# Gated attention and low-rank mixer on one core: batch 0 turns other score blocks by DMA, and the loads of the weights and of batch 1 are placed anew

## The chip, the core and the metric

The kernel runs on one core of one Trainium2 chip. The metric is the device time of one execution in microseconds (us). The engines are TensorE (PE; its weight loads are listed as PEld), VectorE (DVE), ScalarE (ACT), GpSimd (POOL) and SyncE (SP). SP, ACT and POOL also issue DMAs, each in the order of its own queue.

## The reference

Eight batches of 3136 rows. The first stage is attention without a softmax: scores of z with itself, rectified and squared, times v, gated by u. The second is a mixer: a low-rank product along the sequence, then a two-layer network along the channels, each added back.

```python
scores = (1.0 / S) * np.matmul(z, z.transpose(0, 2, 1))   # z: (8, 3136, 64)
attn = np.maximum(scores, 0.0) ** 2                       # symmetric
x = u * np.matmul(attn, v)                                # u, v: (8, 3136, 256)
xt = x.transpose(0, 2, 1)
h = xt @ U @ V                                            # U: (3136, 32), V: (32, 3136)
u2 = x + h.transpose(0, 2, 1)
out = u2 + np.maximum(u2 @ w_ch1, 0.0) @ w_ch2            # 256 -> 1024 -> 256
```

## The kernel before

**Tiles and blocks.** The 3136 rows are 24 tiles of 128 rows and a tail of 64, called tile 24. A score *block* is 128 rows by 128 columns in bf16 (32 KB); `q` holds 296 of them (`NBLK`). For output tile c the kernel needs the blocks (j, c) of all j: 24 matmuls of 128x256 (L1053, `av`) into one PSUM bank, `acc`. The tail's output is 50 smaller matmuls (L1068), turned into shape by one more (L1078). VectorE then gates the result with u into `xc` (L1086, `gate`): this is the *output* of the tile. The outputs of a batch have positions 0 to 24; the tail's stands at position `AT24`.

**How a block is made.** `score` (L1025) multiplies pieces of zT (z transposed, kept twice over the partitions) into a PSUM `pair` of 1024 columns; ACT (L1040) or DVE (L1042) rectifies it into `q`; DVE squares it (L1046). One such piece is a *unit*. Since the scores are symmetric, (c, j) can also be had by turning (j, c): SP issues a DMA transpose (L1049, `q<-q`; `q<-TJ` for the tail). There are three pairs and two accumulators.

**Batch 0** starts cold, and works in groups of four tiles; `DIRECT` gives the limit of each group. A tile c makes its row up to the limit, in pieces of at most 8 blocks, and turns these blocks; the blocks with a tile at or beyond the limit are made twice, once for each side. Groups that `DIRECT` does not name have the limit 24: everything is turned. For the first group the limit is 0: each pair of rows j is made for its four columns at once, the rows from 4 up to `FLIP` are also turned (*flips*), and the blocks beyond `FLIP` are made when that tile comes. Later batches turn everything.

**Mixer.** Each batch's mixer runs beside the next batch's attention: `t1` (L1095, with U), `t1s` (L1112), `h` (L1133, with V), the sum u (L1144), its cast to `ubf` and a DMA transpose to `uT` (L1161), `w1` (L1171), its rectification (L1182, L1184), `w2` (L1197, L1190), the output sum (L1209) and the store (L1214, POOL).

**Loads.** For batch 0, SP and ACT load z (L898, tail L902) and SP most of v (L940); half of v comes by POOL as bf16 (L947), after a one-element copy (L953) that waits for the cast of v that `GATE_V` names. From batch 1 on, all loads are issued by ACT: z in four pieces (cast at L912 and L914 into two buffers `zbf`, the tail in `zbt`, then DMA transposes at L923 into `zT`), v in 13, u in 13 (L967, tail L970). The weights are loaded once by ACT: U at L984 and L988, V at L993, w1 at L978, w2 at L981. Each load has a *gate*, an output of the batch before (of batch 0, for the weights) after which it may go; the numbers are positions. `WAT` gives those of the weights, `Z_AT` the first of z; v starts at position 9. A load from batch 1 on, or of a weight, also takes one of four tokens (`tok`) for as long as the planner thinks it in flight.

**The order** of the whole program is written before it runs, by a planner in Python (`make_plan`, `Plan.run`). It plays a list schedule with costs for each task and emits each engine's instructions in the order so found. `T_BLK` and `T_ROW` are its prices of a transposed block and of a loaded row tile. On PE, `select` takes units of up to `LOOK` positions ahead of the output that is being made, first `av` tasks in their order, and mixer tasks whenever these have fallen behind by `HOLD` (in the last batch `HOLD_LAST`) of a batch. On the chip the engines keep this order and wait for what they need; a wrong price in the planner becomes a wait.

Of the kernel before, what the change touches and what calls it, by code (L numbers as in the profile page):

```python
# [17 lines left out]
NT = 24  # L18
# [4 lines left out]
NBLK = 296  # L23
NXC = 7
NPAIR, NACC = 3, 2
LOOK = 8


DIRECT = (0, 16, 20)

WAT = [(n, 3 + k // 3) for k, n in enumerate((8, 9, 10, 11, 0, 1, 2, 3, 4, 5, 6, 7))]
Z_AT = 5
GATE_V = 1

FLIP = 12
SOFT = 5
NEAR = 2
ACCS = 3
AT24 = 4
HOLD = 0.03  # L40
HOLD_LAST = 0.16

# [52 lines left out]


L_PE, L_EW, L_TR, L_DMA = 0.36, 0.08, 1.3, 2.2  # L100
T_BLK, T_ROW = 0.2, 0.37


class Plan:
# [203 lines left out]
def make_plan():  # L308
    pl = Plan()
    for name, n in (  # L310
        ("xc", NXC), ("pair", NPAIR), ("acc", NACC), ("stg", 6), ("us", 3),
        ("zbf", 2), ("zT", 2), ("v", 2), ("TJ", 1), ("o24", 1), ("u24", 1), ("x24", 2), ("u32", 3), ("ubf", 1), ("uT", 2),
        ("r1", 7), ("r24", 1), ("ob", 2), ("t1", 2), ("t1f", 1), ("tok", 4),
    ):
        pl.pool(name, n)
    pl.free_at["DVE"] = 1.5
# [3 lines left out]
    after = lambda b, pos: out_done.get((b, pos))  # L320
    wts = [[] for _ in range(12)]
    tok = lambda on: [Ref("tok")] if on else []
# [5 lines left out]
    for b in range(NB):  # L328
# [4 lines left out]
        for p, (z0, nb) in enumerate(pieces):  # L333
            st, zbf = Ref("stg"), Ref("zbf")
            ld = add(
                f"zld{b}.{p}", {"ACT": 0.5} if b else {("SP", "ACT")[p % 2]: 0.45},
                lambda K, t, b=b, z0=z0, nb=nb, st=st: K.load_z(t, b, z0, nb, st),
                deps=[after(b - 1, Z_AT + p)] if b else [], prio=0.45 if b else 0.1 * p, pipe=0.1 * nb,
                alloc=[st] + tok(b), behind=zl[-1:],
            )  # L340
            zl.append(ld)
            c0 = flex(add(
                f"zc{b}.{p}0", {"ACT": t_act(64 * nb), "DVE": t_dve(64 * nb)},
                lambda K, t, z0=z0, nb=nb, st=st, zbf=zbf: K.cast_z(t, z0, nb, st, zbf, 0),
                deps=[ld], prio=2 if b else 0, use=[st], alloc=[zbf],
            ), 0.1)
            c1 = flex(add(
                f"zc{b}.{p}1", {"DVE": t_dve(64 * nb), "ACT": t_act(64 * nb)},
                lambda K, t, z0=z0, nb=nb, st=st, zbf=zbf: K.cast_z(t, z0, nb, st, zbf, 1),
                deps=[ld], behind=[c0], prio=2 if b else 0, use=[st, zbf],  # L350
            ), 0.1)
            if b:
                ztr.append(add(
                    f"ztr{b}.{p}", {"SP": t_tr(nb)},
                    lambda K, t, z0=z0, zbf=zbf, zT=zT: K.tr_z(t, z0, zbf, zT),
                    deps=[c0, c1], behind=ztr[-1:], prio=1, pipe=T_BLK * nb,
                    alloc=[] if p else [zT], use=[zbf, zT] if p else [zbf],
                ))
            else:

                pr = Ref("pair")
                m = add(
                    f"zt{b}.{p}", {"PE": 0.06 * nb}, lambda K, t, z0=z0, nb=nb, zbf=zbf, pr=pr: K.mm_z(t, z0, nb, zbf, pr),
                    deps=[c0, c1], kind="z", alloc=[pr], use=[zbf],
                )
                ztr.append(flex(add(
                    f"ze{b}.{p}", {("ACT", "DVE")[p % 2]: (t_act, t_dvp)[p % 2](P * nb)},
                    lambda K, t, z0=z0, nb=nb, pr=pr, zT=zT: K.copy_z(t, z0, nb, pr, zT),
                    deps=[m], behind=ztr[-1:], prio=0, alloc=[] if p else [zT], use=[pr, zT] if p else [pr],
                )))  # L370
# [3 lines left out]
        for n, k in enumerate([12] + list(range(12))):  # L374
            if b == 0 and 6 <= k < 12:

                if k % 2 == 0:
                    if k == 6:

                        c = add(  # L380
                            f"vg{b}", {"POOL": 0.1}, lambda K, t, v=v: K.gate_v(t, v),
                            deps=[vc[GATE_V]], prio=0.1, use=[v], lat=0.1,
                        )
                        vgate = [c]
                    c = add(
                        f"vx{b}.{k}", {"POOL": 0.6}, lambda K, t, k=k, v=v: K.load_v_bf(t, k, v),
                        deps=vgate, behind=[vc[k - 1]] if k > 6 else [], prio=0.2, pipe=T_ROW * 4, use=[v],
                    )
                vc[k] = c
                continue  # L390
            st = Ref("stg")
            w = 2 if k < 12 else 1
            ld = add(
                f"vld{b}.{k}", {"ACT": 0.5} if b else {"SP": 0.5},
                lambda K, t, b=b, k=k, st=st: K.load_v(t, b, k, st),
                deps=[after(b - 1, 9 + n)] if b else [],
                prio=(0.45 if b else 0.3) + 0.001 * n, pipe=T_ROW * w, alloc=[st] + tok(b), behind=vl[-1:] or (zl if b == 0 else []),
            )
            vl.append(ld)
            c = flex(add(  # L400
                f"vc{b}.{k}", {"DVE": t_dve(256 * w), "ACT": t_act(256 * w)},
                lambda K, t, k=k, st=st, v=v: K.cast_v(t, k, st, v),
                deps=[ld], behind=list(vc.values())[-1:], prio=4, use=[st, v] if n else [st], alloc=[] if n else [v],
            ))
            vc[k] = c
# [5 lines left out]
        sq, row, tr, col = {}, {}, {}, {}  # L411
        TJ = Ref("TJ")
        order = list(range(NT))
        order.insert(AT24 if b else 4, NT)
        place = {c: n for n, c in enumerate(order)}

        def split(c, t0, n):
# [18 lines left out]
        for c in range(NT):  # L436
            units += later.pop(c, [])
            lim, s = NT, c // 4
            if b == 0 and s < len(DIRECT):
# [7 lines left out]
                at, n = place[far] if far < NT else 0, NT - far  # L447
# [7 lines left out]
        for at, lim, parts, *j0 in units:  # L455
# [12 lines left out]
            else:  # L468
# [27 lines left out]
                deps=[it], prio=1.0, use=refs,  # L496
# [4 lines left out]
                deps=[it.relu], prio=0.9, use=refs,  # L501
            )
            x = None
            if nt:
# [4 lines left out]
                    deps=[s], prio=0.5, pipe=T_BLK * nt, use=src + tb.refs, lat=L_TR + (1.0 if b == 0 and c >= 8 else 0.0),  # L509
# [23 lines left out]
        for pos, c in enumerate(order):  # L533
            if c == NT or c % 2 == 0:
# [3 lines left out]
                    deps=[after(b, pos - 6) if pos > 6 else after(b - 1, 18 + pos)] , prio=3.5 if b or pos > 6 else 0.4, behind=[] if b else vl[-1:],  # L538
                    pipe=T_ROW * 2, alloc=[u] + tok(b or pos > 6),
# [5 lines left out]
            else:  # L545
# [3 lines left out]
                n = 2 if b == 0 and c < 4 else 5  # L549
# [16 lines left out]
            for i, seg in enumerate(groups):  # L566
                deps = {id(d[0]): d[0] for d in seg}
# [7 lines left out]
                if c == NT:  # L575
# [3 lines left out]
                    deps=list(deps.values()) + [last], kind="av", lat=L_PE if end and not (two and c % 2 == 0) else 0.0,  # L579
# [9 lines left out]
            if two and c % 2 == 0:  # L589
# [4 lines left out]
                    deps=[last, sq[NT, c], vc[12], vc[13]], kind="av", lat=L_PE,  # L594
# [3 lines left out]
            if c == NT:  # L598
# [4 lines left out]
                    deps=[last], prio=0.2, alloc=[o24], use=[acc],  # L603
# [4 lines left out]
                    deps=[oc], kind="z", alloc=[acc], use=[o24],  # L608
# [8 lines left out]
            for c, acc, _, done, u, x, uld in gates:  # L617
# [3 lines left out]
                    deps=[done, uld] + ([] if c == NT or c % 4 == 0 else [evs[-1]]) + ([quads[c ^ 2][3]] if quad else []), prio=0.2,  # L621
# [5 lines left out]
            for n in [n for n, at in WAT if at == pos] if b == 0 else ():  # L627
                st = Ref("stg")
                for g in range(4 if n == 10 else 3 if n == 11 else 1):
                    ld = add(  # L630
                        f"wld{n}.{g}", {"ACT": 0.5 if n < 10 else 0.4}, lambda K, t, n=n, g=g, st=st: K.load_w(t, n, g, st),
                        deps=[ev], behind=[] if g == 0 else [ld], prio=0.45, pipe=0.8 if n < 8 else 0.5 if n < 10 else 0.2,
# [4 lines left out]
                        lambda K, t, n=n, g=g, st=st: K.cast_w(t, n, g, st), deps=[ld], prio=5, use=[st],  # L637
                    )))
        if b == 0:
# [4 lines left out]
        t1 = Ref("t1")  # L644
# [3 lines left out]
            deps=evs + need(8, 9), kind="mix", alloc=[acc], use=xs + [x24],  # L648
# [8 lines left out]
        t1f = Ref("t1f")  # L657
        t1c = flex(add(
            f"t1c.{b}", {"ACT": t_act(D), "DVE": t_dvp(D)}, lambda K, t, acc=acc, t1f=t1f: K.t1c(t, acc, t1f),
            deps=[t1m], prio=0.1, alloc=[t1f], use=[acc],  # L660
# [4 lines left out]
            deps=[t1c, repl], kind="z", alloc=[acc], use=[t1f],  # L665
# [3 lines left out]
            deps=[t1s], prio=0.1, alloc=[t1], use=[acc],  # L669
        ), 0.2)  # L670
        hs = []
        for k in (0, 2, 4, 6):
# [3 lines left out]
                lambda K, t, k=k, prs=prs, t1=t1: K.hmm(t, k, prs, t1),  # L676
                deps=[t1d] + need(10), kind="mix" if b < NB - 1 or k > 0 else "z", use=[t1], **takes(prs + us), behind=[hs[-1][0]] if hs else [],
# [5 lines left out]
        for k in range(7):  # L683
# [6 lines left out]
                lambda K, t, k=k, pr=pr, x=x, u32=u32: K.uadd(t, k, pr, x, u32),  # L690
                deps=[hm], prio=0.6, use=[pr, x] + refs_of(u32),
# [3 lines left out]
                lambda K, t, k=k, u32=u32, ubf=ubf: K.ucast(t, k, u32, ubf),  # L695
                deps=[ua], prio=0.7, use=refs_of(u32), behind=lastc, **takes([ubf]),
# [4 lines left out]
                lambda K, t, k=k, ubf=ubf, uT=uT: K.utr(t, k, ubf, uT),  # L701
                deps=[uc], prio=0.3, pipe=T_BLK * (1 if tail else 2 * w), use=refs_of(ubf), behind=lastt, **takes([uT]),
# [3 lines left out]
            for g in range(1 if tail else 4):  # L706
                pr, r1 = Ref("pair"), Ref("r24" if tail else "r1")
# [3 lines left out]
                    lambda K, t, k=k, g=g, pr=pr, uT=uT: K.w1(t, k, g, pr, uT),  # L711
                    deps=[ut] + need(0, 1, 2, 3), kind="mix", alloc=[pr, r1], use=refs_of(uT), behind=lastw + ws[-1:],
                )
                n = 512 if tail else 1024
# [3 lines left out]
                    deps=[m], prio=0.8, use=[pr, r1],  # L718
# [552 lines left out]
```

## Time and profile before

| | |
|---|---|
| median of 4 runs | 1044.18 us (1042.63 to 1047.44) |
| the profiled execution | 1047.44 us, span 1045.7 us |
| PE busy | 1014.0 us, 97% of the span |
| PEld / DVE / ACT / POOL busy | 750.2 / 589.7 / 492.5 / 70.6 us |
| mean granted TensorE clock | 0.994 |
| DMA moved | 177.86 MB, mean 170 GB/s |
| chain that ended last | PE 86%, DMA 8%, DVE 3% of the span |

The profile is of one execution. *Busy* is the time in which an engine has an instruction running; PE's matmuls at half clock count as busy too. A line such as `PE acc L1053` names the engine, the tile that it writes and the line of the kernel; `ACTq` and `SPq` are instructions of these engines' sequencers, DMA issues above all. `DMA a<-b` is a transfer, from its issue to its landing. The DMA share is the mean busy share of the core's 16 DMA engines; it adds up the packets' own times, so that it can pass 1.

### The profile page before, as it was taken

Reading aid. Unit: us, or ns where it says so; the run is one execution under the profiler, and the core shown is the slowest. Engines: PE = TensorE matmul, PEld = TensorE weight load, DVE = VectorE, ACT = ScalarE, POOL = GpSimd, SP = SyncE. Lnnn points to the kernel's source line nnn. Section 1 sums busy time; section 2 is a strip of 40 time slices with the busy share of each in tenths; the row PEclk is TensorE's granted clock in tenths of the full one; section 3 lists DMA queues with packets and bytes.
Section 4 is the critical chain, followed back from the end, with each engine's and each line's share of the span. In section 5 each row is a group of like instructions: output and inputs, shape, how many; then the busy total and the mean of one; then the engine's idle time right before and its main releaser. Section 6 shows DMA issues by size and latency. Waiting matters only on the chain.

```text
span 1045.7 us, 22251 instructions
## 1 busy us (share of the span) xinstructions
PE 1014.0 (97%) x9120; PEld 750.2 (72%) x9193; DVE 589.7 (56%) x1063; ACT 492.5 (47%) x613; POOL 70.6 (7%) x137
## 2 busy tenths in 40 slices
PE   8798999999999999999999999999999999999998
PEld 5566667777777777777677776777777777677765
DVE  7784855546454565555555556555556555543252
ACT  7452544454544545535544445425454454443353
POOL 1310000000000000000000010000000001000000
PEclk9899999999999999999999999999999999999999
DMA  9899999797899897889989788988789898753052
GB/s 199 143 218 197 193 199 224 171 194 141 166 203 197 163 178 170 184 193 181 152 194 191 183 167 171 216 183 179 154 164 209 182 180 165 137 133 88 33 123 86
DMA packets 414183, 177.86 MB, mean 170 GB/s; under 512 B 375904, under 2 KB 379296, under 8 KB 414080
## 3 DMA queue, kind: packets, MB, share of 16 engines
q1 hardware_dynamic: 373072, 96.91, 55.9%
q10 hardware_dynamic: 33408, 56.25, 21.5%
q0 software_dynamic: 7600, 23.27, 7.2%
q8 instruction: 72, 1.18, 0.5%
q14 instruction: 31, 0.25, 0.1%
HBM read 60.70 MB, written 25.69 MB: 83 GB/s over the span
## 4 chain that ended last, share of the span: by engine, by line
PE 86%; DMA 8%; DVE 3%; issue 1%; ACT 1%; ACTq 1%; SPq 0%; DVEq 0%
PE acc L1053 44%; PE acc L1197 15%; PE pair L1171 15%; PE pair L1025 7%; DMA q<-q 3%; DMA uT<-ubf 2%; PE acc L1063 2%; PE acc L1068 1%; DMA zT<-zbf 1%; DMA zT<-zbt 1%; PE pair L1133 1%; DVE q L1046 1%; DMA uT<-ubt 1%; PE acc L1095 1%; PE acc L1190 1%
## 5 line engine op out<-in xcount | busy, mean ns | idle before, releaser
L1053 PE MATMUL acc<-v,q 128*128 128x256 bf16 x4632 | 571.6, 275 | 0.5 <-DMA q<-q 0.5
L1053 PEld LDWEIGHTS <-q 128*128 128x128 bf16 x4632 | 442.3, 98 | 119.4 <-issue 46.2
L1040 ACT ACTIVATE q<-pair 128x1024 bf16<-128x1024 f32 (+7 forms) x271 | 217.2, 848 | 226.3 <-PE pair L1025 198.1
L1182 ACT ACTIVATE r<-pair 128x1024 bf16<-128x1024 f32 (+1 forms) x194 | 187.8, 1011 | 189.2 <-PE pair L1171 172.7
L1046 DVE TENSOR_TENSOR q<-q 128x1024 bf16<-128x1024 bf16 (+7 forms) x400 | 212.7, 570 | 17.5 <-ACT q L1040 16.5
L1086 DVE TENSOR_TENSOR xc<-acc,us 128x256 bf16<-128x256 f32 x192 | 80.8, 421 | 187.3 <-PE acc L1063 94.3
L1197 PE MATMUL acc<-w2b,r 128*128 128x256 bf16 x1536 | 181.2, 273 | 0.3 <-DVE xc L1086 0.3
L1171 PE MATMUL pair<-uT,w1b 128*128 128x512 bf16 (+1 forms) x717 | 163.5, 350 | 6.3 <-DMA uT<-ubf 1.2
L1197 PEld LDWEIGHTS <-r 128*128 128x128 bf16 x1536 | 149.3, 98 | 22.8 <-issue 3.5
L1042 DVE TENSOR_SCALAR q<-pair 128x768 bf16<-128x768 f32 (+6 forms) x129 | 122.8, 958 | 72.9 <-PE pair L1025 63.4
L1171 PEld LDWEIGHTS <-w1b 128*128 128x128 bf16 x896 | 78.9, 98 | 74.0 <-issue 6.1
L1025 PE MATMUL pair<-zT 64*128 64x512 bf16 (+3 forms) x968 | 101.2, 312 | 11.9 <-ACT q L1040 6.4
L1209 DVE TENSOR_TENSOR ob<-acc,u 128x512 f32<-128x512 f32 (+1 forms) x91 | 59.9, 659 | 89.9 <-PE acc L1197 89.1
L1214 POOL DMA_DIRECT2D out_dram<-ob x84 | 45.7, 544 | 870.9 <-DVE ob L1209 731.3
L1025 PEld LDWEIGHTS <-zT 64*128 64x128 bf16 x968 | 36.4, 95 | 44.2 <-issue 29.9
L1144 DVE TENSOR_TENSOR u<-pair,xc 128x1024 f32<-128x1024 f32 x42 | 49.9, 1216 | 12.4 <-PE pair L1133 12.2
L888 ACT CAST ubf<-u 128x1024 bf16<-128x1024 f32 x23 | 24.0, 1045 | 51.5 <-DVE u L1144 49.4
L888 ACT CAST v<-stg 128x512 bf16<-128x512 f32 (+1 forms) x37 | 22.2, 603 | 14.2 <-DVE q L1046 8.7
L1063 PE MATMUL acc<-v,q 64*128 64x256 bf16 (+1 forms) x168 | 28.0, 276 | 0.5 <-DVE ob L1209 0.5
L892 DVE CAST v<-stg 128x512 bf16<-128x512 f32 (+1 forms) x61 | 24.5, 406 | 6.0 <-DMA stg<-in_v_dram 5.9
L912 ACT ACTIVATE zbf<-stg 128x512 bf16<-128x512 f32 (+1 forms) x31 | 18.0, 614 | 18.9 <-DMA stg<-in_z_dram 7.7
L892 DVE CAST ubf<-u 128x1024 bf16<-128x1024 f32 x19 | 13.1, 689 | 18.5 <-DMA uT<-ubf 18.5
(74 smaller groups left out, 243.2 us busy)
## 6 DMA issues: line engine op xcount, KB each, us to landing
us<-in_u_dram ACTq DMA_DIRECT2D x93, 256.0 KB, 3.7
stg<-in_v_dram ACTq DMA_DIRECT2D x84, 256.0 KB, 3.6
out_dram<-ob POOLq DMA_DIRECT2D x84, 256.0 KB, 3.5
q<-q SPq DMA_TRANSPOSE x370, 4.0
stg<-in_z_dram ACTq DMA_DIRECT2D x22, 256.0 KB, 3.3
out_dram<-ob SPq DMA_DIRECT2D x12, 256.0 KB, 2.0
stg<-in_moe_w_ch_dram ACTq DMA_DIRECT2D x8, 256.0 KB, 4.1
stg<-in_v_dram SPq DMA_DIRECT2D x6, 256.0 KB, 4.1
```

The source lines that it names most:

```text
L1025: self.nc.tensor.matmul(out=ps[:, h, pc : pc + w], lhsT=z[a, r * P : (r + 1) * P], rhs=z[a, c0 : c0 + w], start=True, stop=True,)
L1040: self.nc.scalar.activation(out=o, in_=i, func=AF.Relu)
L1042: self.nc.vector.tensor_single_scalar(out=o, in_=i, scalar=0.0, op=ALU.max)
L1046: self.nc.vector.tensor_tensor(out=o, in0=o, in1=o, op=ALU.mult)
L1053: self.nc.tensor.matmul(out=self.acc[acc.i][:, d0 : d0 + D], lhsT=self.q[:, ref.i, :], rhs=self.v[v.i][:, j, :], start=first and n == 0, s ...
L1063: self.nc.tensor.matmul(out=a[:, :D], lhsT=q[r], rhs=v[r, NT + n, :], start=n == 1, stop=n == 0)
L1086: self.nc.vector.tensor_tensor(out=o, in0=i0, in1=i1, op=ALU.mult)
L1144: self.nc.vector.tensor_tensor(out=o, in0=i, in1=x, op=ALU.add)
L1171: self.nc.tensor.matmul(out=o, lhsT=self.w1b[:, e, ht * P : (ht + 1) * P], rhs=r, start=e == 0, stop=e == ND - 1)
L1182: self.nc.scalar.activation(out=o, in_=i, func=AF.Relu)
L1197: self.nc.tensor.matmul(out=self.acc[acc.i][:, w * D : (w + 1) * D], lhsT=self.r1[r1s[ht // 2].i][:, ht % 2, (2 * h + w) * P : (2 * h + w ...
L1209: self.nc.vector.tensor_tensor(out=o, in0=i, in1=x, op=ALU.add)
```

## The change

In batch 0 other blocks are turned by DMA and other blocks are made twice: the flips reach up to tile 16 instead of 12; the limits of the groups of tiles 4 to 7, 8 to 11 and 12 to 15 are 20, 16 and 20 instead of 16, 20 and 24. The tail's output stands at position 6 of batch 0 instead of 4. The gates move: the weights' from positions 3 to 6 to 5 to 8; those of batch 1's z from 5 on to 7 on; those of batch 1's v stand 0.8 positions apart instead of 1. The later batches keep theirs. Tokens are six instead of four. Score units may be 10 positions ahead instead of 8. POOL's loads of v wait for the first cast of a pair of v tiles instead of the second. The planner's prices of a transposed block and of a loaded row tile fall, and so does `HOLD_LAST`.

```diff
-LOOK = 8
-DIRECT = (0, 16, 20)
-WAT = [(n, 3 + k // 3) for k, n in enumerate((8, 9, 10, 11, 0, 1, 2, 3, 4, 5, 6, 7))]
-Z_AT = 5
-GATE_V = 1
-FLIP = 12
-AT24 = 4
-HOLD_LAST = 0.16
+LOOK = 10
+DIRECT = (0, 20, 16, 20)
+FLIP = 16
+WAT = [(n, 5 + k // 3) for k, n in enumerate((8, 9, 10, 11, 0, 1, 2, 3, 4, 5, 6, 7))]
+Z_AT, V_AT = (7, 5), (9, 9)
+V_STEP = (0.8, 1.0)
+GATE_V = 0
+LOADS = 6
+AT24 = (6, 4)
+HOLD_LAST = 0.14
...
-T_BLK, T_ROW = 0.2, 0.37
+T_BLK, T_ROW = 0.18, 0.3
...
-        ("r1", 7), ("r24", 1), ("ob", 2), ("t1", 2), ("t1f", 1), ("tok", 4),
+        ("r1", 7), ("r24", 1), ("ob", 2), ("t1", 2), ("t1f", 1), ("tok", LOADS),
...
-                deps=[after(b - 1, Z_AT + p)] if b else [], prio=0.45 if b else 0.1 * p, pipe=0.1 * nb,
+                deps=[after(b - 1, Z_AT[b > 1] + p)] if b else [], prio=0.45 if b else 0.1 * p, pipe=0.1 * nb,
...
-                deps=[after(b - 1, 9 + n)] if b else [],
+                deps=[after(b - 1, V_AT[b > 1] + int(n * V_STEP[b > 1]))] if b else [],
...
-        order.insert(AT24 if b else 4, NT)
+        order.insert(AT24[b > 0], NT)
```

More of the change, by code (lines that the diff above doesn't have):

```diff
@@ L25 @@
 NPAIR, NACC = 3, 2
-LOOK = 8
-DIRECT = (0, 16, 20)
-WAT = [(n, 3 + k // 3) for k, n in enumerate((8, 9, 10, 11, 0, 1, 2, 3, 4, 5, 6, 7))]
-Z_AT = 5
-GATE_V = 1
-FLIP = 12
-SOFT = 5
-NEAR = 2
-ACCS = 3
-AT24 = 4
+LOOK = 10
[7 more added lines that the diff above has]
+AT24 = (6, 4)
+SOFT, NEAR, ACCS = 5, 2, 3
 HOLD = 0.03
-HOLD_LAST = 0.16
+HOLD_LAST = 0.14
 class Ref:
```

## The prediction, made before the change was run

> **What bounds the kernel now.** I read the windows first. Each row gives the stretch and its length, then busy time and count for PE, PEld, DVE, ACT and POOL, the granted clock, the DMA share and GB/s:
> ```profile
> 30.00:40.00 10.00, 6.58 (x91) 4.86 (x91) 5.77 (x14) 2.93 (x6) 0.00 (x0) 1.00 1.00 168
> 40.00:50.00 10.00, 8.62 (x53) 5.73 (x53) 8.30 (x15) 3.83 (x6) 7.78 (x15) 0.66 0.74 143
> 90.00:100.00 10.00, 5.95 (x69) 4.38 (x67) 4.13 (x13) 1.65 (x3) 0.00 (x0) 0.94 1.08 211
> 100.00:110.00 10.00, 10.00 (x79) 6.79 (x78) 8.68 (x16) 5.64 (x8) 0.00 (x0) 0.89 1.15 203
> ...
> 0.00:160.00 160.00, 141.44 (x1277) 100.62 (x1280) 112.80 (x218) 81.72 (x109) 18.41 (x41) 0.97 1.04 193
> 160.00:320.00 160.00, 158.78 (x1422) 118.38 (x1433) 89.52 (x160) 78.78 (x104) 9.76 (x18) 1.00 0.93 182
> ```
> Over the whole span PE is busy 1014.0 of 1045.7 us. The first 160 us hold 18.6 us of its 31.7 idle, four of them before the first data; each later 160 us holds 1 to 2, the last 86 us 7.3. Batch 0 is the stage with something to win or lose, with two holes (30 to 50, 90 to 110) that also cost clock (0.66, then 0.94 and 0.89).
>
> PE's waits in the first 170 us name both holes:
> ```profile
> PE pair L1025 <- ACT q L1040: 6.4, 8, 2.4
> PE pair L1025 <- DMA zT<-zbt: 4.0, 1, 4.0
> ```
> The chain, in order of time (start, length), shows what stands behind them:
> ```profile
> 35.09 5.51 DMA q<-q
> 40.62 0.32 ACTq L993
> 41.04 0.82 ACT q L1040
> 41.90 0.40 PE pair L1025
> 42.31 5.47 PE acc L1053 x25
> ...
> 77.33 9.72 DMA zT<-zbf
> 87.15 0.35 ACTq L940
> ...
> 89.72 8.96 DMA zT<-zbt
> 98.72 1.42 PE pair L1025 x26
> 100.14 3.87 PE acc L1053 x25
> ```
> Hole 1: ACT is idle 70% of 30 to 40 us, yet PE waits for its eviction. The step before that eviction is no arithmetic but ACT issuing a load of V (L993), 0.02 us after a *transpose* landed. In the records each issue on SP or ACT carries one of eight completion semaphores and goes out only when that semaphore's last DMA has landed. So ACT, holding the next load, stands until an SP transpose ahead of it lands, with evictions queued behind the load: 1.76 us at 34.0 to 35.8 (load of U), 1.70 at 37.3 to 39.0 and 0.22 at 40.4 (V). PE stands 2.39 + 0.95 us. The next 25 matmuls take 5.47 us where the timeline has 2.84 for 25 at full clock.
> Hole 2: batch 1's first score panel needs all of zT. The second z transpose takes 9.72 us, a v load (L940) holds ACT 5.67 us until it lands, the third cast of z stands behind both, and the last z transpose lands at 98.68. PE waits 4.05 us and runs at half clock from 98.81 to 102.22.
>
> **The change, part by part.**
> *Work.* A tile's row makes its own blocks up to its group's limit and turns them by DMA; blocks beyond are made twice. Turned blocks by group of four tiles, now: 32 (flips of tiles 4 to 11), 38, 38, 38, 22, 6 = 174 in 4+8+8+8+4+3 = 35 DMAs. After: 48, 54, 22, 22, 22, 6 = 174 in 6+8+4+4+4+3 = 29. Score blocks are 402 either way, so PE, eviction and transpose volumes stay; the *when* moves. Units fall from 64 to 56.
> *Eight evictions and squares fewer.* ACT's eviction takes 1022 ns for 1024 columns and 816 for 768: some 0.20 us fixed. The squares, 684 and 583 ns, give 0.28. 8 x 0.48 = 3.8 us of ACT and DVE. PE's waits on these two in batch 0 outside hole 1 are 6.4 - 3.34 + 0.8 + 1.0 = 4.9 us; an eighth of that is -0.6 (ends 0 and -3.8).
> *Turned earlier.* 16 flips and 16 blocks of tiles 4 to 7 come in addition between 11 and 45 us. The packets under 512 B of SP's queue before 120 us took 60.2 us of all 16 engines for 269 blocks: 0.22 us a block, 7.2 us in all. U and V leave that stretch: 784 KB at 1.16 us per 256 KB (ACT's packets, 45.3 us for 10.2 MB), 3.6 us. Net 3.6 more, of which the free quarter of DMA at 40 to 50 us takes 2.6: +1.0 (ends 0 and +3.6). From tile 8 on there are 32 fewer blocks and 8 fewer transposes ahead of the z transposes in SP's queue.
> *Weights two outputs later* (outputs 5 to 8 instead of 3 to 6). U and V leave the time when tiles 4 to 7 are turned; the 10 issues that held ACT go out after output 5, which is near 47 us now. The deadlines are far: U is used at 118.9, V at 125.2, w1 at 138.3; POOL's casts of V take 15.2 us and end near 72 instead of 57. Hole 1 closes: 2.39 + 0.95 + (5.47 - 2.84) = -6.0 (ends 0 and -6.0: the loads may meet other slow transposes).
> *Batch 1's z at outputs 7 to 10 instead of 5 to 8; its v still from 9, the last at 18 instead of 21.* Hole 2 is 4.05 us plus half of 3.41 lost to the clock, 5.75. Fewer transposes ahead shorten the z path; later loads and denser v loads lengthen it. I take half: -2.9 (ends -5.75, and +8.6 as in the slow rival).
> By the trace a hole of 2.39 us was enough for half clock from 40.78 to 47.61. The Trainium skill (TensorE: Matmul & The Clock Gate, Part 1: The HAM clock gate) lets the clock fall only after an idle window of about 3.4 us. By that rule a hole 2 of 2.0 us would keep full clock and the term would be -3.7; by the row it would not, and the term would be -2.0.
> *Six loads at once instead of four.* With eight semaphores, six loads leave two slots for transposes before someone stands. Such waits reached PE as holes of 0.51 us (at 54.4) and 2.39: I add one of their mean, +1.5 (ends 0 and +5.75, a second hole 2).
> The Trainium skill (DMA: Bandwidth & Descriptors, Issuing engines are not separate DMA queues) speaks against this part: all queues share the same 16 engines, so more loads in flight bring no bandwidth. The DMA share of 1.08 at 90 to 100 us agrees; by that rule alone hole 2 would not shrink and the sum would be -4.1.
> *Panels 10 ahead, the planner's lower DMA prices (T_BLK, T_ROW), HOLD_LAST 0.14.* These hold in all batches. PE idles 6.2 us in 160 to 960, its longest hole there 0.79: 0 taken, ends -3 and +5.6 (one such hole in each of seven batches). The last batch's hold moves mixing by a fiftieth of a batch; 990 to 1000 us has 1.4 us idle, so 0, ends -1.4 and +1.4.
> *Batch 0's tail tile after tile 5, GATE_V 0.* The tail's 50 matmuls (1.62 us) fill PE while tile 4's blocks turn; they stay ready, and the planner takes the first ready output, so 0 (if that cover went, +1.6). The three POOL loads of v wait for a cast ending at 8.82 instead of 9.77: 0, ends -1 and +1.
>
> Sum: -6.0 - 2.9 - 0.6 + 1.0 + 1.5 = -7.0 us. The profiled execution took 1047.44 us (span 1045.7), so 1040.4; it lies 3.26 above the median of the four runs, 1044.18, so the forecast is **1037.2**.
>
> **Rivals.** A measurement tells about 0.3%, 3.1 us, from no change: faster is under 1041.1, slower over 1047.3.
> *Both holes close:* -6.0 - 5.75 - 0.6 + 1.0 + 1.5 = -9.9, 1034.3; without the two costs 1031.8. For it: both hang on late DMAs, and 8 transposes leave. Against: the share stays near 1.
> *It does not do what it says:* batch 1 is not loaded later. The gate of its first z load opened at 42.0 us (tile 4's output), yet the load went out at 62.17, after the weights; it waited for a place among four loads, not for its gate. With six places and the weights bunched after output 5, loads meet the remaining transposes at 47 to 60 us and hole 1 moves there: -6.0 + 6.0, hole 2 as it was, -0.6 + 1.0 = +0.4, 1044.6.
> *Slower: z comes too late.* Hole 2 ends when the last z transpose lands. Two outputs are 8.6 us here (47.22 to 55.80); if z truly comes that much later while panels 10 ahead put batch 1 no later into PE's order, hole 2 grows by 8.6: -6.0 + 8.6 - 0.6 + 1.0 + 1.5 = +4.5, 1048.7. It decides from a growth of 7.2 on (7.2 - 4.1 = 3.1); with hole 1 open too it is 1054.7. For it: the z path has two buffers and landings of 9 to 10 us with v loads beside it, which now begin with it. Against: the z loads waited 20 us after their gate anyway.
>
> **How the numbers follow.** Forecast (hole 1 gone, hole 2 about halved) 0.43, its own range 1033 to 1041; both closed 0.17; nothing moved 0.13; slower 0.27. Faster 0.60, same 0.13, slower 0.27. A low end of 1030 takes in the second rival case and a little of the unknowns elsewhere; 1050 takes in the slow one at its own price and leaves out its worse half.
>
> **What would show it.** Right: ACT has no load issue between 32 and 40 us, PE's idle at 38 to 42 is gone and the clock row of 40 to 50 reads 1.00; q transposes in batch 0 number 29; the wait for zT falls to about 2 us; 160 to 960 keeps some 6 us idle. Wrong: PE still waits on evictions with a load issue before them, only later; the wait for zT is over 7 us; or new holes after 160 us, where I put nothing.

## The result, and the profile after

The changed kernel takes 1044.43 us (median of 43 runs, 1039.54 to 1051.20); the kernel before, on the same chips, 1046.28 (64 runs, 1036.00 to 1053.04). The ratio is 0.9991, 95% interval 0.9978 to 1.0004: -0.9 us, no change that this measurement can tell, where -7 us had been forecast. The profiled execution took 1047.67 us, span 1045.9.

The windows of the changed kernel, in stages of 160 us (columns as in the prediction), and below the dots two of the kernel before:
```profile
0.00:160.00 160.00, 143.55 (x1297) 102.39 (x1301) 115.88 (x207) 83.87 (x113) 19.98 (x43) 0.98 0.98 199
160.00:320.00 160.00, 157.49 (x1418) 117.52 (x1430) 91.64 (x172) 73.49 (x92) 9.16 (x17) 1.00 0.91 183
...
480.00:640.00 160.00, 156.82 (x1469) 115.88 (x1476) 93.09 (x167) 69.64 (x84) 10.00 (x18) 0.99 0.89 171
640.00:800.00 160.00, 157.12 (x1406) 116.94 (x1419) 90.48 (x160) 79.37 (x100) 9.56 (x17) 1.00 0.89 178
...
480.00:640.00 160.00, 159.08 (x1501) 118.59 (x1511) 88.89 (x160) 76.20 (x95) 10.28 (x19) 1.00 0.89 176
640.00:800.00 160.00, 159.01 (x1414) 117.06 (x1426) 94.67 (x170) 77.90 (x95) 9.91 (x18) 1.00 0.88 183
```
PE is busy 2.1 us longer in the first stage than before (143.55 against 141.44), and less busy in three later stages: 157.5, 156.8 and 157.1 of 160 us where the windows of before had 158.8 to 159.1; in the other two, from 320 and from 800 us, it is busy 0.6 and 1.2 us longer. What the first stage gained came back as idle time after it. PE's waits in the whole execution name both sides (the last line is the kernel before's):
```profile
PE pair L1171 <- DMA uT<-ubf: 6.6, 3, 2.6
PE acc L1053 <- DVE xc L1086: 4.8, 3, 2.0
PE pair L1025 <- ACT q L1040: 4.2, 5, 2.9
...
PE pair L1171 <- DMA uT<-ubf: 1.2, 3, 0.8
```
The wait for zT (4.0 us before) is gone; waits for uT (1.2 before) have come. The wait for evictions is still there, at another time. Its chain:
```profile
41.07 4.26 DMA q<-q
45.33 0.02 issue
45.35 0.33 ACTq L993
...
45.77 0.28 ACT o L888
46.05 0.04 issue
46.09 0.33 PE acc L1078
...
51.34 6.22 DMA q<-q
...
57.63 0.34 ACTq L967
...
58.93 1.03 ACT q L1040
59.96 0.04 issue
60.00 0.45 PE pair L1025 x2
```
This is hole 1 again, link for link: a transpose lands, the load issue that ACT stood at goes out within 0.1 us (first a load of V, then one of u), the instruction that PE needs follows on ACT (first the copy of the tail's output, then an eviction), and PE goes on. It has moved from 38 us to 45 and 57.

### The profile page after: what moved, and what is told of

Its sections match the earlier page's. It is cut to its first block, busy times and chain, and to the rows that moved or that the text cites. A ratio compares the mean times of both kernels' runs of the same rounds, so it can differ in the third digit from the quotient of the medians.

```text
span 1045.9 us, 22175 instructions
## 1 busy us (share of the span) xinstructions
PE 1012.1 (97%) x9103; PEld 748.5 (72%) x9177; DVE 597.6 (57%) x1064; ACT 486.0 (46%) x596; POOL 72.2 (7%) x137
## 2 busy tenths in 40 slices
DMA packets 413990, 177.84 MB, mean 170 GB/s; under 512 B 375712, under 2 KB 379104, under 8 KB 413888
## 4 chain that ended last, share of the span: by engine, by line
PE 90%; DMA 5%; DVE 3%; issue 1%; ACT 1%; ACTq 0%; SPq 0%; DVEq 0%
PE acc L1053 46%; PE acc L1197 16%; PE pair L1171 16%; PE pair L1025 7%; PE acc L1063 2%; DMA uT<-ubf 2%; DMA q<-q 1%; DVE q L1046 1%; PE acc L1068 1%; DMA zT<-zbf 1%; PE pair L1133 1%; PE acc L1190 1%; DMA stg<-in_v_dram 1%; PE acc L1095 1%; DVE q L1042 0%
## 5 line engine op out<-in xcount | busy, mean ns | idle before, releaser
L1053 PE MATMUL acc<-v,q 128*128 128x256 bf16 x4632 | 573.6, 274 | 5.4 <-DVE xc L1086 4.8
L1053 PEld LDWEIGHTS <-q 128*128 128x128 bf16 x4632 | 441.9, 98 | 124.8 <-issue 50.7
L1040 ACT ACTIVATE q<-pair 128x1024 bf16<-128x1024 f32 (+6 forms) x263 | 214.5, 862 | 226.2 <-PE pair L1025 205.6
L1046 DVE TENSOR_TENSOR q<-q 128x1024 bf16<-128x1024 bf16 (+6 forms) x392 | 210.8, 578 | 13.7 <-ACT q L1040 12.7
L1197 PE MATMUL acc<-w2b,r 128*128 128x256 bf16 x1536 | 183.6, 274 | 0.0
L1171 PE MATMUL pair<-uT,w1b 128*128 128x512 bf16 (+1 forms) x716 | 165.8, 350 | 10.3 <-DMA uT<-ubf 6.6
L1042 DVE TENSOR_SCALAR q<-pair 128x768 bf16<-128x768 f32 (+6 forms) x129 | 125.0, 974 | 53.7 <-PE pair L1025 50.3
L1025 PE MATMUL pair<-zT 64*128 64x384 bf16 (+3 forms) x952 | 100.6, 314 | 5.3 <-ACT q L1040 4.2
L892 DVE CAST v<-stg 128x512 bf16<-128x512 f32 (+1 forms) x69 | 28.2, 408 | 21.8 <-DMA stg<-in_v_dram 20.9
L1171 PE MATMUL pair<-q,w1b 128*128 128x512 bf16 (+1 forms) x106 | 22.0, 351 | 1.6 <-DVE q L1144 1.0
L1040 ACT ACTIVATE TJ<-pair 128x1024 bf16<-128x1024 f32 (+1 forms) x10 | 9.4, 947 | 23.1 <-DVE xc L1086 16.1
```

The source lines that it names most:

```text
L1025: self.nc.tensor.matmul(out=ps[:, h, pc : pc + w], lhsT=z[a, r * P : (r + 1) * P], rhs=z[a, c0 : c0 + w], start=True, stop=True,)
L1040: self.nc.scalar.activation(out=o, in_=i, func=AF.Relu)
L1042: self.nc.vector.tensor_single_scalar(out=o, in_=i, scalar=0.0, op=ALU.max)
L1046: self.nc.vector.tensor_tensor(out=o, in0=o, in1=o, op=ALU.mult)
L1053: self.nc.tensor.matmul(out=self.acc[acc.i][:, d0 : d0 + D], lhsT=self.q[:, ref.i, :], rhs=self.v[v.i][:, j, :], start=first and n == 0, s ...
L1171: self.nc.tensor.matmul(out=o, lhsT=self.w1b[:, e, ht * P : (ht + 1) * P], rhs=r, start=e == 0, stop=e == ND - 1)
```

## The experiments

The ratios are to runs of the kernel before, made beside them on the same chip. For the traces three figures serve throughout, worked out from PE's records: *lost* is the sum of PE's gaps over 0.15 us and half of the time at half clock; the mark is the start of `t1` of batch 1, by which batch 0 is over whatever was interleaved; *rest* is from there to the end. A row's trace is one execution, and it can be far from its kernel's median: that of `before_redraw` took 1043.50 us, the lowest of 12 with a median of 1050.44.

| kernel | ratio (95%) | lost 8-70 | lost 70-120 | lost 160-960 | mark | rest |
|---|---|---|---|---|---|---|
| before | 1 | 9.7 | 8.0 | 2.9 | 248.7 | 797.0 |
| before_again | 0.9996 (0.9967-1.0026) | 8.8 | 6.7 | 3.1 | 245.1 | 796.4 |
| after | 0.9991 (0.9978-1.0004) | 10.8 | 4.1 | 8.3 | 245.7 | 800.2 |
| after_again | 0.9997 (0.9972-1.0023) | 10.1 | 4.7 | 3.9 | 241.4 | 797.8 |
| before_pool | 1.0017 (0.9991-1.0043) | 7.8 | 9.5 | 2.9 | 248.3 | 795.7 |
| after_pool | 0.9985 (0.9960-1.0011) | 5.9 | 15.8 | 3.2 | 248.8 | 795.4 |
| before_thin | 0.9951 (0.9924-0.9977) | 8.1 | 0.8 | 4.5 | 238.7 | 798.7 |
| after_thin | 0.9972 (0.9948-0.9995) | 12.1 | 1.6 | 3.8 | 242.7 | 796.4 |
| b0_only | 1.0036 (1.0008-1.0065) | 7.2 | 9.5 | 8.5 | 249.6 | 798.3 |
| glob_only | 1.0200 (1.0162-1.0239) | 11.5 | 17.8 | 10.4 | 257.4 | 803.7 |
| T_only | 1.0157 (1.0115-1.0199) | 9.2 | 13.8 | 8.7 | 250.8 | 803.3 |
| LOOK_only | 1.0029 (0.9998-1.0059) | 9.8 | 9.4 | 3.3 | 249.7 | 797.2 |
| after_oldT | 0.9958 (0.9931-0.9984) | 9.1 | 3.1 | 5.7 | 241.2 | 798.4 |
| after_oldT_again | 0.9964 (0.9939-0.9988) | 7.5 | 2.3 | 4.7 | 237.9 | 797.3 |
| after_T20_30 | 1.0005 (0.9982-1.0028) | 9.2 | 7.6 | 4.4 | 242.9 | 798.3 |
| after_T22_37 | 1.0003 (0.9978-1.0028) | 8.3 | 6.2 | 9.6 | 245.6 | 801.4 |
| after_T16_25 | 1.0075 (1.0044-1.0105) | 4.3 | 5.3 | 16.5 | 243.9 | 803.8 |
| oldT_fewer | 1.0039 (1.0011-1.0067) | 11.4 | 0.9 | 10.5 | 246.0 | 797.8 |
| before_redraw | 1.0065 (1.0038-1.0091) | 7.8 | 4.3 | 5.9 | 241.2 | 800.5 |
| after_redraw | 1.0052 (1.0027-1.0076) | 16.5 | 6.5 | 2.8 | 247.2 | 797.1 |

**Is a profile's hole the kernel's, or the execution's?** Both kernels once more, unchanged.

> The kernel before, unchanged, profiled once more. If its two holes belong to the order: PE waits 2 us or more for an eviction near 38 us and about 4 us for zT near 95, t1 of batch 1 within 2 us of 248.7. If they belong to the one execution: holes elsewhere or of other sizes, t1 of batch 1 off by more than 2 us. The time: ratio 1.000 to itself within 0.3%.

> The changed kernel, unchanged, profiled once more. If its holes belong to the order: 1.4 us near 44.7, 2.9 near 56, and waits for uT near 206, 571 and 700 us that sum to some 6.6. If to the one execution: batch 0's holes alike in place but not in size, the uT waits elsewhere or gone. Time: ratio to before within 0.3% of 0.9991.

PE's waits in the first 170 us of the second execution of the kernel before:
```profile
PE pair L1025 <- ACT q L1040: 5.2, 7, 1.6
PE pair L928 <- DVE zbf L914: 4.0, 1, 4.0
PE pair L1025 <- DMA zT<-zbt: 3.3, 1, 3.3
```
The holes belong to the order, their sizes do not. The hole of 2.39 us at 38 is 0.73 at 40.7 here, with 1.58 at 51.7; the zT wait is 3.3 instead of 4.05; the mark comes 3.6 us earlier. The half clock that the prediction put down to hole 1 (40.8 to 47.6) lies at 29.4 to 36.2 this time, ahead of that hole. In the changed kernel's second execution the uT waits at 568 and 695 us stand again (1.3 and 1.7 instead of 2.6 and 2.2), the one at 206 is gone. First execution against first, second against second, the mark gained 3.0 and 3.7 us, and the rest gave back 3.2 and 1.4. That gain is no larger than what one kernel's mark differs by between its own two executions, 3.6 and 4.3 us.

**ACT's standing taken away.** Same order, but the loads of the weights, of batch 0's later u and of batch 1's z and v are issued by POOL.

```diff
+        if t.eng == "ACT" and (t.name[:3] == "wld" or t.name[:4] in ("uld0", "zld1", "vld1")):
+            return self.nc.gpsimd
```

> The kernel before, same order, but the loads of the weights, of batch 0's later u and of batch 1's z and v are issued by POOL instead of ACT. Theory A (ACT stands behind a load issue until a transpose lands, and its evictions behind it): ACT's gaps at 34 to 41 and at 81 to 87 us go, the wait of PE at 38 to 42 us (3.3 us) and the half clock after it (2.6 us) go, hole 2 shrinks: batch 0 ends 5 to 9 us earlier, and the time falls by as much, to 1036 to 1040. Rival B (the DMA engines are full, so that transposes and z come late whichever queue issues the loads): PE's holes stay within 2 us of 12.6 in all between 8 and 120 us, and the time is within 3 us of before. POOL's casts of V (15 us) lie in the same queue and may hold loads back.

> The changed kernel with the same loads issued by POOL instead of ACT. Theory A: the waits of PE at 44.7 (1.4 us) and 56.2 (2.9 us) and the half clock from 60.2 to 63.6 go; batch 0 ends 4 to 6 us earlier than in the changed kernel. Rival B: within 2 us of the changed kernel.

In the kernel before, ACT stood some 20 us at load issues in batch 0; here under 4. PE's hole at 38 to 42 us is gone. The time is not better in either kernel. PE's waits in the first 170 us show where it went (the lines of this kernel stand two further down, L1055 is the old L1053):
```profile
PE acc L1055 <- DMA q<-q: 4.7, 2, 4.4
...
PE pair L1027 <- ACT q L1042: 3.9, 6, 2.3
```
and the chain, which transfer it was:
```profile
77.96 3.47 PE acc L1055 x31
81.43 10.62 DMA q<-q
92.05 0.05 issue
92.10 2.13 PE acc L1055 x11
```
PE's longest wait is no longer for an eviction behind a load; it is for a transpose itself, which lands 10.62 us after 81.4. (The wait of 2.3 us for an eviction, at 115.6, is behind a load of u that stayed with ACT.) In the changed kernel the zT wait came back with 6.93 us. The windows of 80 to 90 us, the kernel before first, and its loads of v show what was in flight:
```profile
80.00:90.00 10.00, 9.51 (x88) 8.30 (x86) 3.86 (x12) 3.02 (x5) 0.00 (x0) 1.00 1.17 172
...
80.00:90.00 10.00, 7.41 (x67) 6.16 (x64) 3.03 (x9) 1.76 (x4) 3.05 (x6) 1.00 1.23 264
```
In the kernel before ACT issued no load from 79 to 87.1 us; here six loads of v went out from 79.3 to 83.7, and the DMA engines moved 264 GB/s instead of 172. So theory A had the link right and the price wrong: ACT's standing kept loads back, and without it they crowd the transposes.

**Less for the DMA engines.** Same order again, half of batch 1's v left out.

```diff
-                out=s.rearrange("p (t d) -> p t d", d=D), in_=self.rows("v", b, 2 * k, 2 * k + 2)
+                out=s.rearrange("p (t d) -> p t d", d=D)[:, : (1 if b == 1 else 2), :], in_=self.rows("v", b, 2 * k, 2 * k + (1 if b == 1 else 2))
```

> The kernel before, same order, but each of the twelve paired v loads of batch 1 fetches one row tile instead of two (half of batch 1's v is left out, the buffer keeps older data): 1.57 MB less between 62 and 108 us, some 7 us of the 16 DMA engines at 1.16 us per 256 KB. Theory B (batch 0 is bound by the DMA engines; where the wait shows is secondary): hole 2 shrinks or goes, t1 of batch 0 starts 4 to 8 us earlier than 118.9 and the time falls by about as much, 1037 to 1041. Rival A (ACT's standing behind load issues, the two buffers of z): t1 moves by less than 2 us, as the number and order of the issues are the same.

> The changed kernel, same order, with half of batch 1's v left out in the same way as in the kernel before (12 loads of one row tile instead of two). Theory B (the DMA engines set batch 0 in both kernels, the holes only show where): t1 of batch 1, at 245.7 in the changed kernel, comes 3 to 8 us earlier, and the time falls by 3 to 6 us, to 1038 to 1041 where before is 1044 to 1046. Rival (in the changed kernel the transfers of batch 0 are spread well enough, and what is left is ACT's standing and the waits for uT): within 2 us of the changed kernel.

The kernel before gains 0.49%, and its zT wait falls to almost nothing, with ACT standing about as long as ever (18.2 us):
```profile
PE pair L1025 <- DMA zT<-zbt: 0.4, 1, 0.4
```
With buffers, queue and order unchanged, 1.57 MB less of other transfers were enough to end hole 2: the last two z transposes took 5.8 and 5.5 us, where the kernel before had 10.0 and 9.0. The changed kernel's gain over itself is 0.19 to 0.25% by the ratios, which the intervals do not separate from none; its hole at 56.7 us even measured 4.03. There the first half of batch 0 is what is left, and those loads run after it.

The third lever was fewer turned blocks, 142 instead of 174, on the changed kernel:

```diff
-DIRECT = (0, 20, 16, 20)
+DIRECT = (0, 16, 16, 20)
-FLIP = 16
+FLIP = 12
-T_BLK, T_ROW = 0.18, 0.3
+T_BLK, T_ROW = 0.2, 0.37
```

> The changed kernel with the old DMA prices, limits 16, 16 and 20 for the groups of tiles 4 to 15, and flips up to 12: 142 blocks of batch 0 are turned instead of 174, and 32 more are made on PE. Less 7.2 us of the DMA engines (0.22 us a block), more 1 us of PE and some 5 us of ACT and DVE. Theory B: 3 to 6 us below the same kernel with 174 turned blocks (ratio to before 0.996), so 1034 to 1037 where before is 1045. Rival (evictions are what batch 0 lacks): as much above it, 1042 to 1046.

1.0039 (1.0011 to 1.0067), 0.8% slower than the same prices with 174 turned blocks (0.9958). The theory of the DMA engines had 1034 to 1037 us; 1045.73 was measured. This speaks against the DMA engines as the only limit, but the order is a new one, and what that alone does is measured below.

**The change in two parts.** What concerns batch 0 and its loads, and what holds in all batches (the six tokens are counted with the first part, but they hold for the loads of every later batch too):

```diff
 # b0_only, against the changed kernel (glob_only: the other way round, against the kernel before)
-LOOK = 10
+LOOK = 8
-HOLD_LAST = 0.14
+HOLD_LAST = 0.16
-T_BLK, T_ROW = 0.18, 0.3
+T_BLK, T_ROW = 0.2, 0.37
 # T_only, against the kernel before
-T_BLK, T_ROW = 0.2, 0.37
+T_BLK, T_ROW = 0.18, 0.3
 # LOOK_only, against the kernel before
-LOOK = 8
+LOOK = 10
```

> The changed kernel with LOOK 8, the planner's old DMA prices and HOLD_LAST 0.16: only what concerns batch 0 and its loads (FLIP, DIRECT, tail position, gates, tokens, GATE_V) is changed. Theory 1 (the settings for all batches gave back what batch 0 won): t1 of batch 0 starts about 3.5 us earlier than before, as in the changed kernel (115.4 against 118.9), the waits for uT between 160 and 960 us are 1 to 2 us instead of 6.6, and the time is some 3 us below the kernel before, 1041. Rival (each newly written order has its own holes, whatever set it off): the time is within 2 us of before or above it, and the lead of batch 0 is not the 3.5 us either, since the batch's order is written anew with the old prices.

> The kernel before with only LOOK 10, the lower DMA prices and HOLD_LAST 0.14. Theory 1: batch 0 keeps both of its holes (PE idle from 8 to 120 us about 12.6 us), 160 to 960 us idles about 10 us instead of 6.2 with waits for uT, and the time is 2 to 5 us above before. Rival: within 2 us of before, no more waits for uT than before.

> The kernel before with only the planner's lower DMA prices (T_BLK 0.18, T_ROW 0.3). Theory (the lower prices bunch the transfers of batch 0 when gates, tokens and limits are the old ones): most of the 22 us that the three settings for all batches cost together appear here, 1058 to 1068, with t1 of batch 0 near 128 us instead of 118.9. Rival (LOOK 10 is what costs): within 4 us of before.

> The kernel before with only LOOK 10. Theory of the prices: within 4 us of before. Rival (panels 10 ahead put more transposes ahead of those of z and u in SP's queue, and these come late): 1058 to 1068, with longer waits for zT and uT.

The theory that settings for all batches took back what batch 0 won is too simple: neither part is faster alone. The part for batch 0 is 0.36% slower, the other part 2.0%, and together they are even. Neither of the expectations for the second part had so much; the better of them put 2 to 5 us. Most of the 2.0% are the lower DMA prices (1.57%). In T_only's trace they cost 6 to 7 us between 70 and 120 us and near 6 after 160 us: six waits for uT of over half a microsecond, from 142 us on, where the kernel before has one. LOOK 10 alone is 0.3% slower, at the edge of its interval.

**The prices on the changed kernel.** Two theories are set against each other. *Theory 3*: the two lower prices are what costs, and the more so the lower they are, since transfers that the planner takes for cheaper than they are get bunched. *Lottery*: each newly written order has its own holes, whatever the price.

```diff
-T_BLK, T_ROW = 0.18, 0.3
+T_BLK, T_ROW = 0.2, 0.37   # after_oldT, after_oldT_again
+T_BLK, T_ROW = 0.2, 0.3    # after_T20_30
+T_BLK, T_ROW = 0.22, 0.37  # after_T22_37
+T_BLK, T_ROW = 0.16, 0.25  # after_T16_25
```

> The changed kernel with the old DMA prices (T_BLK 0.2, T_ROW 0.37). If the lower prices are what makes the new limits and gates pay: t1 of batch 0 comes 4 to 8 us later than in the changed kernel (115.4) and the time is 4 to 8 us above it, 1048 to 1052. If the prices harm on the chip as in the run of the three settings: 1038 to 1042.

> The changed kernel with the old DMA prices, once more. If it is really faster: ratio to before 0.993 to 0.998, as the first time (0.9958). If the first time was luck of the executions: 0.998 to 1.003.

> The changed kernel with only the price of a turned block put back (T_BLK 0.2, T_ROW 0.3). Theory 3: 1040 to 1044. Lottery: anywhere from 1035 to 1050.

> The changed kernel with T_BLK 0.22, which is what a turned block takes of the 16 engines by the packets (0.22 us), and T_ROW 0.37. Theory 3: no worse than with 0.2, 1036 to 1041. Lottery: anywhere from 1035 to 1050.

> The changed kernel with both prices lower still (T_BLK 0.16, T_ROW 0.25). Theory 3: worse than the changed kernel, 1046 to 1056. Lottery: anywhere from 1035 to 1050, as likely below the changed kernel as above.

With both old prices the changed kernel is faster than the kernel before: 0.9958, and 0.9964 when run again. It is ahead of the changed kernel too, less clearly: 1040.98 us against 1043.27, run side by side the second time. The other price pairs gave 1.0005 (0.9982 to 1.0028), 1.0003 (0.9978 to 1.0028) and 1.0075 (1.0044 to 1.0105). The lowest prices are the slowest, and their trace has its loss after batch 0 (16.5 us lost from 160 to 960); yet 0.22 is no better than 0.18, and theory 3 missed with two of its three ranges. There is no order by price. The pair 0.18 and 0.37 has no result. Waits of the faster version, first execution, first 170 us:
```profile
PE acc L1053 <- DVE xc L1086: 5.5, 3, 3.0
...
PE pair L1025 <- ACT q L1040: 1.6, 4, 0.5
PE pair L1025 <- DMA zT<-zbt: 1.6, 1, 1.6
```
Here the waits for evictions and for zT have both shrunk to 1.6 us (at 50.3 us there is one of 3.0 behind a gating, which its second execution lacks), and the mark comes 7.5 and 7.2 us before that of the kernel before. This is the size that the prediction had for batch 0, but not by its steps: lost time from 8 to 70 us, where hole 1 lay, fell by only 0.6 and 1.3 us, and from 70 to 120 by 4.9 and 4.4.

**What a newly written order does by itself.** One latency in the planner is nudged; no volume, gate, limit or token changes. About half of PE's steps change places (925 of 1889 and 839 of 1881).

```diff
-L_PE, L_EW, L_TR, L_DMA = 0.36, 0.08, 1.3, 2.2
+L_PE, L_EW, L_TR, L_DMA = 0.36, 0.07, 1.3, 2.2   # before_redraw
+L_PE, L_EW, L_TR, L_DMA = 0.36, 0.08, 1.3, 2.3   # after_redraw
```

> The kernel before with the planner's latency of an elementwise step at 0.07 instead of 0.08 us: no volume, gate, limit or token changes, but the order is written anew from batch 0 on. Theory of the draw (each newly written order has its own waits, worth some 0.2 to 0.5% either way): 1040 to 1050 where before is 1045, as likely on either side. Rival (an order written from the same settings takes the same time, so that the scatter seen between single settings is theirs): within 1.5 us of before.

> The changed kernel with the planner's latency of a load at 2.3 instead of 2.2 us, nothing else: again only a newly written order. Theory of the draw: 1039 to 1049 where the changed kernel is 1044. Rival: within 1.5 us of the changed kernel.

Ratios to the kernel before: 1.0065 (1.0038 to 1.0091) and 1.0052 (1.0027 to 1.0076). So both lie clear of their own kernels, by some 6 to 7 us, the size of the whole forecast, while the two kernels run again unchanged gave 0.9996 and 0.9997. Both draws came out slower; two draws do not show how wide the scatter is. In after_redraw's trace hole 1 is 5.39 us at 56.1 and the zT wait 4.43 us at 95.3, where the changed kernel had 2.87 and none. The trace of before_redraw does not show where its time goes: its mark is earlier than in the kernel before (241.2 against 248.7 and 245.1), and only the rest is longer, by 3.5 and 4.1 us, with waits for uT (4.9 us against 1.2); it was the fastest execution of its kernel.

## Why the prediction was wrong, by its own steps

*Turned blocks, evictions, PE's work.* The volumes came out as counted: 8 units fewer (DVE's squares go from 400 to 392), PE's matmul records 9120 to 9103, the DMA packets alike (414183 to 413990), 6 turning DMAs fewer (`q<-q` from 370 to 364). What this was to bring, -0.6, is too small to be told apart.

*Hole 1, -6.0: the step that failed.* It was to close because the loads leave the stretch. They did leave it (the first load of U goes out at 40.2 us instead of 31.8), but they met the next transposes, and PE's waits behind them moved to 45 and 57 us. Lost time from 8 to 70 us is 10.8 and 10.1 us, against 9.7 and 8.8 before: +1.1 and +1.3, where this term makes -4.1 even with the -0.6, +1.0 and +1.5 beside it. The step's own upper end, 0, named this case, and so did the rival in which hole 1 moves (0.13, 1044.6 us). That rival had the mechanism; that its number lies so near 1044.43 is luck in part, since it left hole 2 as it was and put nothing after 160 us. Two of the prediction's signs of being wrong came true: PE waits behind a load issue, only later, and there are new holes after 160 us.

Two sizes in the step were wrong as well. The hole is 2.4 and 0.95 us in one execution and 0.7 and 1.6 in another. And the half clock that was counted with it came also without it: for 6.8 us from 29.4 in before_again, ahead of the hole, and for 6.8 us from 31.1 in before_pool, which has no such hole. Nor did closing it pay there: before_pool lost 1.0 to 1.9 us less from 8 to 70 us and 1.5 to 2.8 more from 70 to 120. The step took the releaser in the chain for the cause.

*Hole 2, -2.9.* Lost time from 70 to 120 us fell by 3.9 and 2.0 us: right in size, but not for its reason, fewer transposes ahead. The z loads went out 3 us later than before (65.3 against 62.2 us), and the last z transpose no sooner (89.98 against 89.72). It landed at 95.1 instead of 98.7 because it was faster, 5.2 us instead of 9.0 (before first):
```profile
zT<-zbt SPq DMA_TRANSPOSE x1, 9.0
...
zT<-zbt SPq DMA_TRANSPOSE x1, 5.2
```
In the kernel before five loads of v went out from 87.1 to 89.2 us, just ahead of it. In the changed kernel ACT stood at such a load for 8.4 us, until 89.5, and kept the others back. That these loads set the pace is what before_thin shows; that the term came out was luck in part. The slow rival, z too late, did not happen.

*Six loads, +1.5; turning earlier, +1.0.* Not told apart from hole 1's move; these waits have the same form. ACT stood some 18 to 20 us in batch 0 in all four executions of the two kernels, so six tokens did not lengthen it. No run here has the six tokens alone. The Trainium skill (DMA: Bandwidth & Descriptors, Issuing engines are not separate DMA queues) says that queues share the same 16 engines; before_pool agrees, and shows it with a price: the same loads on another queue moved PE's wait to a transpose of 10.62 us, at 1.0017.

*Settings for all batches, 0 taken, -3 to +5.6.* After the mark 3.2 and 1.4 us were given back, inside the ends. The 0 rested on how little the kernel before idles there, which says nothing of an order that is written anew; the six tokens, which hold there too, were not counted at all. On the old limits the lower prices alone cost 1.57%.

*What no step held:* the order is written anew for the whole program, also where nothing is meant to change. That alone was worth some +0.6% in each of two draws, as much as the forecast's whole sum. The chance of 0.60 for faster rested on two holes of one execution and allowed nothing for it.

What stays open: why these two orders are better than their redraws, and whether the old prices make the changed kernel faster or merely wrote a good order; no run separates the two. Which of the settings, the tokens or the new order gave back the time after the mark is open as well.

## What to carry to other kernels

Where an order is planned as a whole, change one setting that should not matter and measure the scatter before any gain is priced; here it was some 6 to 7 us in both draws. Before a wait is costed as a gain, take a second profile, and ask what its releaser waits for: here an engine that stood at a load issue behind a late transfer was a symptom, and taking the symptom away moved the wait. Halving a transfer, at an unchanged order, is the experiment that told symptom from cause.

## What was not expected of the hardware

Executions of one order differ by ten microseconds and more (1039.5 to 1051.2 for the changed kernel), and much of this goes with the clock: over its 43 executions, time and mean granted clock (0.991 to 0.998) have a correlation of -0.74, some 1.4 us for each 0.001.

The Trainium skill (TensorE: Matmul & The Clock Gate, Part 1: The HAM clock gate) has the clock fall after an idle window of about 3.4 us. Here it fell between 29 and 34 us in 17 of 20 profiles without one, the longest gap ahead of it from 8 us on being 2.1 us: at 29.4 us for 6.8 us in before_again, where that gap was 0.57 us, and at 30.2 us for 10.2 us in after_oldT_again (0.52). Gaps of 1.97 us (the changed kernel, at 93) and 2.27 us (after_oldT_again, at 90.4) left it at full speed. Idle time alone did not decide it.
